# A two-branch kernel on one core: column tiles moved and filled over six rounds, the matrices of the last pass reordered, row endings deferred

## The chip, the core and the metric

The kernel runs on one core of a Trainium2 chip. A core has five engines that run side by side, each through its own stream of instructions in order: PE (TensorE, matrix products; its weight loads are listed as PEld), DVE (VectorE), ACT (ScalarE), POOL (GpSimd) and SP (SyncE, which here only issues transfers). Engines wait for each other through semaphores; 16 DMA engines move data between HBM and the on-chip memory SBUF. PE writes into PSUM, eight banks of 2 KB a partition. The metric is the device time of one execution in microseconds; lower is better.

## The reference

The inputs give two independent results, set side by side in the output (2048 x 2048, bf16).

```python
# A: 64 segments of 32 rows, each with 8 memory rows carried on
for s in range(n_seg):
    h = concat([mem, x[s]]);  q, k, v = h @ Wq, h @ Wk, h @ Wv      # 32 heads of 128
    p = softmax(where(mask, q @ k.T * scale, -1e9));  o = (p @ v) @ Wo
    mem, out[s] = o[:8], o[8:]
# B: a long convolution, its kernel from 128 complex exponentials per channel
K = einsum('dn,dnl,dn->dl', C, exp(dt*A * l), dt*B).real            # 1024 channels, 2048 lags
y = irfft(rfft(u, 4096) * rfft(K, 4096))[:2048] + u * Dskip
```

Both the kernel's spectra and those of the input `u` are made by matrix products with cosine and sine matrices here, not by an FFT.

## The kernel before, in words

Branch B (`part_b`) runs first, then A (`part_a`). Branch B has four stages.

*Parameters.* Tables of exponents and angles are made; the transform's matrix `MF` and the transposes of A's input are made beside them.

*Rounds.* Loop `f` from -1 to 16 (L1270) runs a list of words, `ORDER`, and each word issues one small step; a prime means "of the round before". Rounds 0 to 15 each treat 64 channels: eight exponentials on ACT (words E0 to E7, tile `E`, from PE's `pa`), turns on DVE (n0 to n7, `nr` from `ptt`), sine and cosine on ACT (S, C), products on DVE (gi, gr), the kernel values on PE (K0, K1) and their copy into `KxT` on DVE (x0, x1). Words P, U and M fill the rest with side work: P are projections of branch A, U are transforms of `u`, M transposes matrices. A run word issues PE's part, its small letter the copy out of PSUM: on ACT for p0, p2, p3, p5, on DVE for p1, p4. Every fourth U copy ends in six additions on POOL (`ux` from `us`) and a store to HBM (`Ud`). The PSUM tiles of this side work, of K and of the later builds come from one pool of four banks (`take`). At round 16 only a closing list runs, `LAST` (L1269), which finishes round 15's values and starts what follows.

*Columns.* `columns_of_turns` (L1042) makes two small tiles, `g_l` and `g_r`, by POOL iotas, memsets and selections and by DVE arithmetic; it is called once, at round 3. In round 15 `turned_columns` (L1101) transposes them on PE and copies them out (`lhs`, `wts`, `rhs`); it takes the place of the projections, so the words P and p issue it. From these `build` (L1122) makes the matrices of one of four row groups `kc`: 14 steps, each one or two products and a sine or copy on ACT; three of the steps are amplitudes (`amp`). `weighted` (L1148) multiplies a half of the matrices by them on DVE. In the closing list G0 runs nine steps for `kc` = 0, G1 weighs the first half, G2 runs the other five and the first spectrum on PE, G3 weighs the second half and runs its spectrum, then issues two loads for block 1.

After the list, the 44 stores of kernel values from `KxT` to HBM (`Kd`) that `late` still holds are issued in turn on SP and POOL (L1329), and the pools of the rounds are closed (L1337): from the constants upward `tabs` (tables, columns, staged tiles), `kxp` (two `KxT`) and `tmp` (the rounds' tiles), and from the other end `up` (tiles of the U side). New pools are opened in the memory that they leave: `mnp`, `iv`, `bp`, `pw` (tiles `y` and `z`) and `bp0` on one side, `a_wre1` (tile `k1`, whose upper part holds the amplitudes of the later builds, and the inverse matrices `MI`) on the other. A pool that takes memory of a closed one waits, at its first use, for whatever still reads there.

*Blocks.* Loop `b` from 0 to 15 (L1458). `pointwise` multiplies the spectrum of the values, from two PSUM tiles `hps`, by that of `u` (`uq`, loaded two blocks ahead) on DVE: four instructions into `z` and `y`, at the second `next` four more, which write `Bt`. Between them PE makes the spectrum of the next block, two halves of 20 products, into `hps` tiles from a pool of three. From block 4 on, `inverses(2)` follows: `inverse` (L1426) makes 32 products from `MI` and `Bt` into `yp` on PE, scales them to `yb` on ACT (two buffers), and then DVE ends the row: `uu` times `Dskip`, plus `yb`. The store of `uu` is put on a list, `unsent`, and issued on ACT's queue in a later `inverse`. The row tiles `uu` are loaded six inverses ahead on SP, nine buffers. Eight inverses are left after the loop. Weights of branch A are loaded beside the blocks as memory comes free.

Branch A then loops over 64 segments with part of its weights resident and the rest streamed (tile `wst`).

All engines follow the order in which the program issues their instructions.

Of the kernel before, what the change touches and what calls it, by code (L numbers as in the profile page):

```python
# [10 lines left out]
BF16 = mybir.dt.bfloat16  # L11
# [651 lines left out]
def part_b(ctx, tc, u, A_re, A_im, B_re, B_im, C_re, C_im, log_dt, Dskip, out_b, ahead, copies, residents, first_state):  # L663
# [378 lines left out]
    def columns_of_turns():  # L1042

        at = tabs.tile([128, 6], I32, name="g_at")
        for j, (b0, step) in enumerate(((0, 2), (256, 2), (512, 4), (1024, 8), (2048, 16), (0, 2))):
            gp.iota(at[:, j:j + 1], pattern=[[1, 1]], base=b0, channel_multiplier=step)
        atF = tabs.tile([128, 6], F32, name="g_atF")
        v.tensor_copy(out=atF[:], in_=at[:])

        def select(t_, dims, fill, base, cm):  # L1050
            gp.affine_select(out=t_, in_=t_, compare_op=ALU.is_ge, fill=float(fill), base=base, pattern=[[0, n_] for n_ in dims], channel_multiplier=cm)
# [4 lines left out]
        v.tensor_copy(out=at[:], in_=atF[:])  # L1056
        hl = tabs.tile([128, 2, 6], I32, name="g_hl")
        v.tensor_scalar(out=hl[:, 0, :], in0=at[:], scalar1=6, scalar2=None, op0=ALU.logical_shift_right)
        v.tensor_scalar(out=hl[:, 1, :], in0=at[:], scalar1=63, scalar2=None, op0=ALU.bitwise_and)
        for i, (lo, n_) in enumerate(((0, 2), (2, 3))):  # L1060
            v.tensor_copy(out=g_l[:, 0:10, lo:lo + n_].rearrange("p (s j) c -> p s j c", s=2),
                          in_=hl[:, i, 0:5].unsqueeze(1).unsqueeze(3).to_broadcast([128, 2, 5, n_]))
            v.tensor_copy(out=g_l[:, 10, lo:lo + n_], in_=hl[:, i, 5:6].to_broadcast([128, n_]))
        gp.memset(g_l[:, 0:11, 5:6], 1.0)
        gp.memset(g_l[:, 0:11, 6:7], 0.25)
        gp.memset(g_l[:, 5:10, 6:7], 0.0)
        pn = tabs.tile([128, 4], I32, name="g_pn")
        gp.iota(pn[:, 0:1], pattern=[[1, 1]], base=0, channel_multiplier=1)
        v.tensor_scalar(out=pn[:, 1:2], in0=pn[:, 0:1], scalar1=1, scalar2=None, op0=ALU.bitwise_and)
        v.tensor_scalar(out=pn[:, 2:3], in0=pn[:, 0:1], scalar1=4, scalar2=None, op0=ALU.logical_shift_right)  # L1070
        v.tensor_scalar(out=pn[:, 3:4], in0=pn[:, 0:1], scalar1=15, scalar2=None, op0=ALU.bitwise_and)
        pnF = tabs.tile([128, 5], F32, name="g_pnF")
        v.tensor_copy(out=pnF[:, 0:4], in_=pn[:])
        gp.memset(g_l[:, 11:14, :], 0.0)
        gp.memset(g_l[:, 11:14, 0:1], 1.0)
        gp.memset(g_l[:, 12:14, 1:2], 2.0)
        gp.memset(g_l[:, 13:14, 2:4], 2.0)
        for i, j in ((0, 1), (1, 2), (2, 4)):
            v.tensor_scalar(out=g_l[:, 11 + i, j:j + 1], in0=pnF[:, 1:2], scalar1=-2.0, scalar2=2.0, op0=ALU.mult, op1=ALU.add)
        select(g_l[:, 11:13, 0:5], (2, 5), 0, -1, 1)  # L1080
        select(g_l[:, 13:14, 4:5], (1, 1), 0, -1, 1)
        gp.memset(g_l[:, 11:13, 5:6], 2.0)
        gp.memset(g_l[:, 12:13, 6:7], 2.0)
        select(g_l[:, 11:13, 5:7], (2, 2), 0, 0, -1)
        kq = tabs.tile([128, 2, 16], I32, name="g_kq")
        gp.iota(kq[:, 0, :], pattern=[[1, 4], [0, 4]], base=0, channel_multiplier=0)
        gp.iota(kq[:, 1, :], pattern=[[0, 4], [1, 4]], base=0, channel_multiplier=0)
        kqF = tabs.tile([128, 2, 16], F32, name="g_kqF")
        v.tensor_copy(out=kqF[:], in_=kq[:])
# [5 lines left out]
        v.tensor_scalar(out=rv[:, :, 4], in0=kqF[:, 1, :], scalar1=1.0 / 8, scalar2=0.0, op0=ALU.mult, op1=ALU.add)  # L1095
        gp.memset(g_r[:, :, :, 5:6], 128.0)
        gp.memset(g_r[:, :, :, 6:7], 1.0)

    G = {}

    def turned_columns():  # L1101

        for i in range(4):
            pt = take([128, 8, 128], BF16, "gt")
            for c in range(8 if i != 1 else 6):
                pe.transpose(out=pt[0:7, c, :], in_=g_l[:, 8 * i + c, :] if i < 2 else g_r[:, 2 * (i - 2) + c // 4, c % 4, :], identity=ident[:])

            def evict(copy, i=i, pt=pt):
                flat = pt[0:7].rearrange("p c n -> p (c n)")
                if i == 0:  # L1110
                    copy(out=G["lhs"][:, 0:1024], in_=flat)
                elif i == 1:
                    copy(out=G["lhs"][:, 1024:1408], in_=flat[:, 0:384])
                    copy(out=G["wts"], in_=flat[:, 384:768])
                else:
                    copy(out=G["rhs"][:, 1024 * (i - 2):1024 * (i - 2) + 1024], in_=flat)
            yield evict

# [147 lines left out]
    for eng, names in ((sc.copy, ON_ACT), (v.tensor_copy, ON_DVE)):  # L1266
        for nm, kind, slot in names:
            evict_of[nm] = (kind, slot, eng)
    LAST = ("w0' b0' C0' b1' gi0' C1' G0 gr0' w1' gr1' gi1' K0' K1' G1 x0' x1' G2 M0 G3 m0").split()  # L1269
    for f in range(-1, 17):  # L1270
        if f == 3:
            columns_of_turns()
        if f == 15:
# [13 lines left out]
        for word in ORDER if f < 16 else LAST:  # L1287
            nm, r = word.rstrip("'"), f - word.endswith("'")
            if f == 16 and nm[0] in "GMm" and not word.endswith("'"):
                if nm == "G0":  # L1290
                    for _ in range(9):
                        next(made)
                elif nm == "G1":
                    weighted(0, 0, amp0)
                elif nm == "G2":
                    for _ in made:
                        pass
                    s0 = ps_e.tile([128, 2, 512], F32, name="pa", tag="pa")
# [127 lines left out]
    def inverse(dq, c, uu, neg, mn):  # L1426
# [11 lines left out]
        sc.activation(out=yb[:], in_=yp, func=ACT.Copy, scale=float(2.0 / PLEN))  # L1438
        while len(unsent) > (1 if len(todo) > 6 else 0):
            unsent.pop(0)()  # L1440
        v.tensor_tensor(out=uu[:], in0=uu[:], in1=Dsk[:, d].unsqueeze(1).to_broadcast([128, 2, DQ]), op=ALU.mult)
        v.tensor_tensor(out=uu[:], in0=uu[:], in1=yb[:], op=ALU.add)
        unsent.append(lambda: sc.dma_start(out=out_v[r][:, mc:mc + 2, d], in_=uu[:]))

# [13 lines left out]
    for b in range(16):  # L1458
# [3 lines left out]
        points = pointwise(b, now)  # L1462
        next(points)
        if b == 0:
            ctx_p.close()
# [214 lines left out]
```

## Time and profile before

| what | value |
|---|---|
| runs | 2044.19, 2046.65, 2042.81 us, median 2044.19 |
| profiled execution | time 2047.62 us, span 2045.9 us, mean PE clock 0.975 |
| PE / DVE / ACT / POOL busy | 1834.5 / 1411.2 / 958.1 / 415.3 us |
| HBM read, written | 528.25 MB, 66.05 MB |

Times in the trace count from the start of the span. An instruction's row gives its start, its duration, engine, line, operation, the tile written and the tile read with their shapes, and in brackets how long the engine stood idle ahead of it and for whom. A row of waits gives the waiting engine and line, the releaser, the total, the number and the longest. A row of groups gives count, busy time and mean nanoseconds. A row of stages gives, for a stretch, each engine's busy time, the granted PE clock (1.00 is full), the share of DMA time and GB/s.

### The profile page before, as it was taken

What the parts mean: (1) busy time and instruction counts of PE and PEld (TensorE: products, weight loads), DVE (VectorE), ACT (ScalarE), POOL (GpSimd) and SP (SyncE); (2) the same over time, 40 slices, a digit from 0 to 9 for tenths busy, and PEclk for the clock granted to TensorE, in tenths of its full rate; (3) what the DMA queues carried; (4) which work ended last, traced back from release to release, by engine and by line L of the source; (5) the groups of instructions that cost most, each with busy time, mean ns of one, the idle gap of its engine ahead of it and who ended that gap; (6) DMA issues with size and microseconds to landing.
All of it is one profiled execution on the core that took longest, in us unless ns stands there. A gap on an engine that the chain in (4) does not pass through costs nothing.

```text
span 2045.9 us, 74541 instructions
## 1 busy us (share of the span) xinstructions
PE 1834.5 (90%) x31928; PEld 1130.4 (55%) x31956; DVE 1411.2 (69%) x3442; ACT 958.1 (47%) x1672; POOL 415.3 (20%) x851
## 2 busy tenths in 40 slices
PE   1698999866999879999999999999999999999998
PEld 1365666644877535555555555555555555555554
DVE  8878999958887346666766667666666666666650
ACT  4887988862222324443444444444434444344430
POOL 2135454442200011111111111111111111111121
PEclk9999999977999979999999999999999999999999
DMA  6787997746446999999999999999999999999991
GB/s 169 185 227 227 274 269 202 200 139 212 158 141 203 316 325 339 340 341 340 344 348 332 339 335 358 344 343 344 350 325 350 342 339 341 345 347 344 345 339 50
DMA packets 348469, 588.69 MB, mean 288 GB/s; under 512 B 109865, under 2 KB 225913, under 8 KB 346089
## 3 DMA queue, kind: packets, MB, share of 16 engines
q1 hardware_dynamic: 294748, 526.35, 76.0%
q10 hardware_dynamic: 44812, 28.26, 4.5%
q0 software_dynamic: 8576, 29.32, 4.0%
q8 instruction: 250, 4.10, 0.8%
q14 instruction: 83, 0.67, 0.1%
HBM read 528.25 MB, written 66.05 MB: 290 GB/s over the span
## 4 chain that ended last, share of the span: by engine, by line
PE 35%; DMA 24%; DVE 4%; issue 1%; ACT 1%; POOL 0%; SPq 0%; POOLq 0%; DVEq 0%; ACTq 0%
PE acc L375 18%; DMA wst<-WD_v 11%; PE pp L488 9%; DMA wst<-WD_o 5%; DMA arena<-PKd 3%; PE pe L625 3%; PE tr L386 2%; DMA wst<-WD_q 2%; DMA wst<-WD_k 2%; PE pv L456 1%; PE pv L460 1%; DVE arena L582 1%; ACT arena L582 1%; PE sc L400 1%; PE tro L588 1%
## 5 line engine op out<-in xcount | busy, mean ns | idle before, releaser
L375 PEld LDWEIGHTS <-a_hT 128*32 128x32 bf16 x12352 | 327.2, 96 | 318.3 <-issue 63.0
L381 ACT CAST arena<-acc 128x512 bf16<-128x512 f32 x384 | 224.7, 585 | 397.6 <-PE acc L375 321.9
L375 PE MATMUL acc<-W,a_hT 128*32 128x512 bf16 x4608 | 334.7, 380 | 2.2 <-issue 1.2
L488 PEld LDWEIGHTS <-arena 128*32 128x32 bf16 x8256 | 216.8, 97 | 86.3 <-issue 62.5
L375 PE MATMUL acc<-wst,a_hT 128*32 128x512 bf16 x2304 | 229.7, 381 | 26.6 <-DMA wst<-WD_v 17.8
L389 POOL COPY arena<-arena 128x128 bf16<-128x128 bf16 x128 | 37.4, 292 | 851.4 <-DMA arena<-PKd 300.3
L296 DVE TENSOR_SCALAR arena<-keep 128x256 int32<-128x256 int32 (+1 forms) x512 | 175.5, 394 | 28.1 <-PE acc L375 26.8
L375 PE MATMUL acc<-gF,a_hT 128*32 128x512 bf16 x2048 | 145.6, 382 | 0.0
L488 PE MATMUL pp<-W_o,arena 128*32 128x256 bf16 x4096 | 139.0, 275 | 6.4 <-DMA W_o<-in_A_Wo_dram 5.1
L168 PE MATMUL pro<-xTl,wsl 128*128 128x512 bf16 x490 | 115.9, 389 | 16.2 <-ACT kst L177 7.9
L415 DVE TENSOR_REDUCE a_mx<-sc 128x4 f32<-128x160 f32 (+1 forms) x192 | 71.6, 373 | 77.5 <-PE sc L403 77.5
L419 ACT ACTIVATE sc<-sc 128x160 f32<-128x160 f32 (+1 forms) x192 | 63.9, 333 | 122.9 <-DVE sc L416 122.1
L503 DVE COPY arena<-tr 128x512 bf16<-128x512 bf16 x64 | 27.2, 425 | 128.3 <-PE tr L386 128.3
L423 DVE TENSOR_REDUCE a_mx<-sc 128x4 f32<-128x160 f32 (+1 forms) x192 | 72.8, 379 | 55.5 <-ACT sc L419 55.1
L1208 ACT ACTIVATE E<-pa 128x648 bf16<-128x648 f32 x128 | 90.9, 710 | 32.2 <-PE pa L1200 27.0
L1423 PE MATMUL yp<-Bt,MI 128*128 128x256 bf16 x680 | 104.6, 273 | 0.7 <-ACT yb L1438 0.7
L450 POOL TENSOR_TENSOR arena<-arena,a_BD 128x128 bf16<-128x128 bf16 x128 | 51.0, 399 | 234.9 <-DVE arena L433 218.5
L168 PEld LDWEIGHTS <-wsl 128*128 128x128 bf16 x512 | 51.1, 100 | 77.7 <-issue 23.3
L582 ACT CAST arena<-pp 128x128 bf16<-128x128 f32 x64 | 17.0, 265 | 161.3 <-DVE arena L582 161.3
L375 PE MATMUL acc<-W_v,a_hT 128*32 128x512 bf16 x1280 | 92.3, 381 | 0.0
L1216 DVE TENSOR_SCALAR nr<-ptt 128x456 f32<-128x456 int16 x128 | 77.3, 624 | 17.7 <-PE ptt L1194 16.0
L386 PEld LDWEIGHTS <-arena 128*128 128x128 bf16 x1024 | 57.8, 98 | 54.5 <-issue 44.9
(311 smaller groups left out, 3866.5 us busy)
## 6 DMA issues: line engine op xcount, KB each, us to landing
wst<-WD_v SPq DMA_DIRECT2D x256, 512.0 KB
wst<-WD_k SPq DMA_DIRECT2D x192, 512.0 KB
wst<-WD_o SPq DMA_DIRECT2D x192, 512.0 KB
wst<-WD_q SPq DMA_DIRECT2D x128, 512.0 KB
Ud<-ux POOLq DMA_DIRECT2D x16, 1024.0 KB, 6.1
uq<-Ud SPq DMA_DIRECT2D x32, 512.0 KB
wsl<-in_A_Wk_dram SPq DMA_DIRECT2D x16, 512.0 KB
wsl<-in_A_Wv_dram SPq DMA_DIRECT2D x16, 512.0 KB
```

Of the source, the lines that this page charges most:

```text
L168: nc.tensor.matmul(a[:], lhsT=w[:, kc, 128 * j:128 * j + 128], rhs=xTl[:, kc, :, :].rearrange("p s k -> p (s k)"), start=(kc == 0), stop=( ...
L296: nc.vector.tensor_scalar(out=out.bitcast(I32), in0=in_.bitcast(I32), scalar1=0, scalar2=None, op0=ALU.bitwise_or)
L375: nc.tensor.matmul(a[32 * g:32 * g + 32, o_:o_ + rhs.shape[1]], lhsT=hT[:, kc, :], rhs=rhs, start=(kc == 0), stop=(kc == KC - 1), tile_pos ...
L381: nc.scalar.copy(out=q, in_=a[:])
L386: nc.tensor.transpose(out=p[:, hl, :, :].rearrange("p a b -> p (a b)"), in_=q[:, 128 * hl:128 * hl + 128], identity=ident[:])
L415: nc.vector.tensor_reduce(out=m_, in_=x, axis=AX.X, op=ALU.max)
L419: nc.scalar.activation(out=flat(sc, i), in_=flat(sc, i), func=ACT.Exp, scale=scale)
L423: nc.vector.tensor_reduce(out=m_, in_=x, axis=AX.X, op=ALU.add)
L488: nc.tensor.matmul(po[32 * qt:32 * qt + 32, o_:o_ + rhs.shape[1]], lhsT=oT[:, h % 4, (h % 16) // 4, :], rhs=rhs, start=False, stop=(h == 3 ...
L1208: sc.activation(out=T["E", r, e // 4][:, lo:lo + 8 * NE].rearrange("p (i c) -> p i c", i=2), in_=T.pop(("p", r, e))[:, :, 0:4 * NE], func= ...
L1216: v.tensor_scalar(out=T["n", r, e // 4][:, lo:lo + 8 * NT], in0=T.pop(("t", r, e))[:, 0:8 * NT].bitcast(I16)[:, 0:16 * NT:2], scalar1=floa ...
L1423: pe.matmul(yp[:, b, :], lhsT=m_[:, b, cs, kc, :], rhs=Bt[:, kc, j, half, c_, :], start=(kc == 0 and cs == 0 and half == 0), stop=(kc == 3 ...
```

## The change

Four things, all in `part_b`.

1. `g_l` and `g_r` and the seven small tiles that feed them leave the pool `tabs` for the pool `up`, on the other side of the memory.
2. `columns_of_turns` becomes a generator of six steps: POOL's constants, DVE's first part, POOL's selections, and three DVE parts; one step is issued at the start of each of rounds 1 to 6. `turned_columns` is no longer run by the words P and p: its six steps follow the words E1 to E6 of round 15, each copy is issued at once, the first two transposed tiles are copied by DVE, the others by ACT in two halves each.
3. The closing list: all 14 build steps at G0, G1 ahead of K0', x0' ahead of K1', and the copy of the last U tile, until now at the end of round 15, behind x1'.
4. In `inverse` the two DVE instructions that end a row become a function, kept in the list `endings`; `end()` runs what is kept behind the first part of the next block's `pointwise`, and in the last eight inverses behind each one. All stores on `unsent` are issued at the next `inverse`.

```diff
-    g_l = tabs.tile([128, 14, 7], BF16, name="g_l")
-    g_r = tabs.tile([128, 4, 4, 7], BF16, name="g_r")
...
+    g_l = up.tile([128, 14, 7], BF16, name="g_l")
+    g_r = up.tile([128, 4, 4, 7], BF16, name="g_r")
...
     def columns_of_turns():
-        at = tabs.tile([128, 6], I32, name="g_at")
...
+        at, pn, kq, hl = (up.tile([128, *dims], I32, name="g_%s" % nm) for nm, dims in (("at", (6,)), ("pn", (4,)), ("kq", (2, 16)), ("hl", (2, 6))))
+        atF, pnF, kqF = (up.tile([128, *dims], F32, name="g_%sF" % nm) for nm, dims in (("at", (6,)), ("pn", (5,)), ("kq", (2, 16))))
         for j, (b0, step) in enumerate(((0, 2), (256, 2), (512, 4), (1024, 8), (2048, 16), (0, 2))):
             gp.iota(at[:, j:j + 1], pattern=[[1, 1]], base=b0, channel_multiplier=step)
...
+        gp.memset(g_r[:, :, :, 6:7], 1.0)
+        yield
         v.tensor_copy(out=atF[:], in_=at[:])
...
+            v.tensor_scalar(out=g_l[:, 11 + i, j:j + 1], in0=pnF[:, 1:2], scalar1=-2.0, scalar2=2.0, op0=ALU.mult, op1=ALU.add)
+        yield
...
         select(g_l[:, 13:14, 4:5], (1, 1), 0, -1, 1)
+        yield
...
     def turned_columns():
...
-            def evict(copy, i=i, pt=pt):
...
-            yield evict
+            if i == 0:
+                v.tensor_copy(out=G["lhs"][:, 0:1024], in_=flat)
+            elif i == 1:
+                v.tensor_copy(out=G["lhs"][:, 1024:1408], in_=flat[:, 0:384])
+                v.tensor_copy(out=G["wts"], in_=flat[:, 384:768])
+            else:
+                for h in range(2):
+                    sc.copy(out=G["rhs"][:, 1024 * (i - 2) + 512 * h:1024 * (i - 2) + 512 * h + 512], in_=flat[:, 512 * h:512 * h + 512])
+                    yield
+                continue
+            yield
...
-    LAST = ("w0' b0' C0' b1' gi0' C1' G0 gr0' w1' gr1' gi1' K0' K1' G1 x0' x1' G2 M0 G3 m0").split()
+    LAST = ("w0' b0' C0' b1' gi0' C1' G0 gr0' w1' gr1' gi1' G1 K0' x0' K1' x1' U3 G2 M0 G3 m0").split()
+    steps = columns_of_turns()
     for f in range(-1, 17):
-        if f == 3:
-            columns_of_turns()
+        if 1 <= f <= 6:
+            next(steps)
...
-            side_ops["P"] = (turned_columns(),)
+            turning = turned_columns()
...
+            if f == 16 and nm == "U3":
+                run_evict("U", 3, v.tensor_copy)
...
                 if nm == "G0":
-                    for _ in range(9):
-                        next(made)
+                    for _ in made:
+                        pass
...
-                if f == 15 and nm == "m":
-                    run_evict("U", 3, v.tensor_copy)
...
+                elif f == 15 and nm in ("E1", "E2", "E3", "E4", "E5", "E6"):
+                    next(turning)
...
-        while len(unsent) > (1 if len(todo) > 6 else 0):
+        while unsent:
             unsent.pop(0)()
...
+        def ending():
+            v.tensor_tensor(out=uu[:], in0=uu[:], in1=Dsk[:, d].unsqueeze(1).to_broadcast([128, 2, DQ]), op=ALU.mult)
+            v.tensor_tensor(out=uu[:], in0=uu[:], in1=yb[:], op=ALU.add)
+            unsent.append(lambda: sc.dma_start(out=out_v[r][:, mc:mc + 2, d], in_=uu[:]))
+        endings.append(ending)
...
+    def end():
+        while endings:
+            endings.pop(0)()
...
         next(points)
+        end()
...
     ctx2.close()
+    end()
     for n_ in range(8):
         inverses(1)
+        end()
```

More of the change, by code (lines that the diff above doesn't have):

```diff
@@ L1045, in columns_of_turns @@
         for j, (b0, step) in enumerate(((0, 2), (256, 2), (512, 4), (1024, 8), (2048, 16), (0, 2))):
             gp.iota(at[:, j:j + 1], pattern=[[1, 1]], base=b0, channel_multiplier=step)
[L1047 to L1051, printed above, removed]
+        gp.iota(pn[:, 0:1], pattern=[[1, 1]], base=0, channel_multiplier=1)
@@ new lines, in columns_of_turns @@
+        gp.memset(g_l[:, 12:13, 6:7], 2.0)
+        select(g_l[:, 11:13, 5:7], (2, 2), 0, 0, -1)
+        gp.memset(g_r[:, :, :, 5:6], 128.0)
+        gp.memset(g_r[:, :, :, 6:7], 1.0)
+        yield
+        v.tensor_copy(out=atF[:], in_=at[:])
+        v.tensor_scalar(out=pn[:, 1:2], in0=pn[:, 0:1], scalar1=1, scalar2=None, op0=ALU.bitwise_and)
+        v.tensor_scalar(out=pn[:, 2:3], in0=pn[:, 0:1], scalar1=4, scalar2=None, op0=ALU.logical_shift_right)
+        v.tensor_scalar(out=pn[:, 3:4], in0=pn[:, 0:1], scalar1=15, scalar2=None, op0=ALU.bitwise_and)
@@ L1052, in columns_of_turns @@
+        v.tensor_copy(out=pnF[:, 0:4], in_=pn[:])
+        v.tensor_copy(out=kqF[:], in_=kq[:])
+        for i, j in ((0, 1), (1, 2), (2, 4)):
+            v.tensor_scalar(out=g_l[:, 11 + i, j:j + 1], in0=pnF[:, 1:2], scalar1=-2.0, scalar2=2.0, op0=ALU.mult, op1=ALU.add)
+        yield
         for j, fill in ((2, 513), (3, 1025), (4, 2050)):
@@ L1095, in columns_of_turns @@
         v.tensor_scalar(out=rv[:, :, 4], in0=kqF[:, 1, :], scalar1=1.0 / 8, scalar2=0.0, op0=ALU.mult, op1=ALU.add)
-        gp.memset(g_r[:, :, :, 5:6], 128.0)
-        gp.memset(g_r[:, :, :, 6:7], 1.0)
+        yield
+        v.tensor_copy(out=at[:], in_=atF[:])
+        v.tensor_scalar(out=hl[:, 0, :], in0=at[:], scalar1=6, scalar2=None, op0=ALU.logical_shift_right)
+        v.tensor_scalar(out=hl[:, 1, :], in0=at[:], scalar1=63, scalar2=None, op0=ALU.bitwise_and)
+        yield
+        for i, (lo, n_) in enumerate(((0, 2), (2, 3))):
+            v.tensor_copy(out=g_l[:, 0:10, lo:lo + n_].rearrange("p (s j) c -> p s j c", s=2),
+                          in_=hl[:, i, 0:5].unsqueeze(1).unsqueeze(3).to_broadcast([128, 2, 5, n_]))
+            v.tensor_copy(out=g_l[:, 10, lo:lo + n_], in_=hl[:, i, 5:6].to_broadcast([128, n_]))
+        yield
     G = {}
@@ L1295, in part_b @@
                 elif nm == "G2":
-                    for _ in made:
-                        pass
                     s0 = ps_e.tile([128, 2, 512], F32, name="pa", tag="pa")
```

61 lines of the change are left out of this document (17 added, 44 removed).

## The prediction

> **What bounds the kernel now.** I read the page's busy shares first, then a table of stages, then the waits and the timeline of each stage that the diff touches.
>
> ```profile
> span 2045.9 us, 74541 instructions
> PE 1834.5 (90%) x31928; PEld 1130.4 (55%) x31956; DVE 1411.2 (69%) x3442; ACT 958.1 (47%) x1672; POOL 415.3 (20%) x851
> ```
> ```profile
> core 0: us, PE busy (x) PEld busy (x) DVE busy (x) ACT busy (x) POOL busy (x), PEclk, DMA share, GB/s
> 200.00:399.90 199.90, 199.13 (x2584) 134.78 (x2595) 186.61 (x291) 178.85 (x201) 101.05 (x122) 1.00 0.85 236
> 404.20:427.00 22.80, 13.61 (x216) 9.28 (x213) 19.27 (x32) 18.97 (x21) 6.35 (x8) 0.85 0.79 255
> 427.00:447.00 20.00, 10.17 (x163) 6.23 (x162) 15.57 (x16) 11.93 (x17) 9.80 (x7) 0.55 0.19 73
> 447.00:467.00 20.00, 12.14 (x67) 6.83 (x66) 0.06 (x1) 10.65 (x21) 11.60 (x21) 0.67 0.30 79
> 526.90:645.90 119.00, 107.24 (x954) 91.18 (x954) 97.10 (x111) 28.98 (x32) 0.00 (x0) 1.00 0.54 167
> 666.00:742.00 76.00, 55.69 (x642) 36.13 (x640) 23.92 (x64) 20.15 (x31) 2.80 (x8) 0.85 0.94 336
> 760.00:2030.00 1270.00, 1211.81 (x25167) 700.18 (x25169) 820.00 (x2561) 510.55 (x1124) 202.15 (x507) 1.00 0.94 334
> ```
>
> In the steady rounds PE has no slack (199.1 of 199.9 us) and DVE 7%, so a delay on DVE reaches PE. In the last round (404 to 427), in the closing pass and the hand-over to the blocks (427 to 467) no engine is full: these are waits. In the blocks with inverses PE has 107 of 119 us. The attention, from 760 on, is untouched and starts when the blocks end. So each stall taken away before 700 us should move the end by its own length, unless the loading at 666 to 742, with the DMA engines 94% busy, eats it.
>
> **The columns over six rounds.** Now all of it stands at the start of round 3:
>
> ```profile
> 157.17 0.68 DVE L946 COPY ms<-mt 128x1024 bf16<-128x1024 bf16 x1
> 159.46 0.17 DVE L1048 CAST g_atF<-g_at 128x6 f32<-128x6 int32 x1 [1.61 <-POOL g_at L1046]
> 160.58 0.17 DVE L1056 CAST g_at<-g_atF 128x6 int32<-128x6 f32 x1 [0.95 <-POOL g_atF L1051]
> 163.21 0.18 DVE L1089 CAST g_kqF<-g_kq 128x32 f32<-128x32 int32 x1 [1.05 <-POOL g_kq L1087]
> 163.73 0.19 DVE L1095 TENSOR_SCALAR g_r<-g_kqF 128x16 bf16<-128x16 f32 x1
> 169.26 3.44 PE L168 MATMUL pro<-xTl,wsl 128*128 128x512 bf16 x8 [4.93 <-ACT kst L177]
> ```
> ```profile
> DVE wn L1234 <- ACT sn L1221: 2.3, 10, 0.2
> ```
>
> DVE waits three times for POOL (3.6 us) and computes 22 small instructions; it is held from 157.85, the end of the copy ahead, to 163.92. PE pays 4.93 us at 169.26. Afterwards POOL's part stands a round ahead, so the three waits go; its 21 instructions in round 1 and 7 selections in round 3 (0.1 to 0.2 us each; POOL is half idle in the rounds) delay only loads of parameters that are used a round later. The DVE instructions stay: about 1.2 us in round 2, 0.6 in round 4, 0.5 in 5, 0.4 in 6, from their starts in the timeline. Each round has 0.2 us free there (the wait for the sine). Since nearly all of the held time reached PE, I charge the rest: 1.0+0.4+0.3+0.2 = 1.9 us. Net **-3.0 us** (ends -4.9, if small pieces vanish in gaps, and -2.0, if they pull further waits along).
>
> **The turned columns in round 15.** 30 transposes and their copies move from the place of the projections to behind the exponentials E1 to E6.
>
> ```profile
> 412.12 0.70 PE L1200 MATMUL pa<-RE,pt 128*128 128x324 bf16 x2 [7.70 <-ACT E L1208]
> L1116 ACT COPY g<-gt 7x1024 bf16<-7x1024 bf16 x2 | 2.0, 984 | 0.0
> L1111 ACT COPY k<-gt 7x1024 bf16<-7x1024 bf16 x1 | 1.0, 984 | 0.0
> L1106 PE MATMUL gt<-b_ident,g_l 128*7 128x128 bf16 x14 | 0.9, 219 | 0.0
> ```
>
> Three copies of 0.98 us stand on ACT ahead of E0, E1 and E2 while PE waits 7.70 us for E0. Moving them starts E0 0.98 us earlier, and ACT is relieved of one copy (DVE takes it; a 1024-column copy takes DVE about 0.7 us). Against it: the 0.9 us of 14 transposes makes some 2.1 us for 30, now between the exponentials, where PE is on the path; DVE and ACT wait in line for each of them, and behind them stand the turns and products of the same round. The last U copy (two DVE instructions of 0.68 us) leaves the round. I take **-1 us** (ends -3 and +2: copies hidden entirely, or transposes all on the path with DVE's waits).
>
> **The closing pass and the hand-over.** These rows carry it:
>
> ```profile
> 430.39 2.18 DVE L1182 TENSOR_TENSOR gi<-E,sn 128x1824 bf16<-128x1824 bf16 x1
> 440.80 1.04 DVE L1015 CAST KxT<-kp 128x392 bf16<-128x392 f32 x2
> 444.38 0.96 DVE L1151 TENSOR_TENSOR g<-g,amp 128x1536 bf16<-128x1536 bf16 x1 [2.55 <-ACT g L1120]
> 466.94 1.22 DVE L1366 TENSOR_TENSOR z<-uq,pa 128x1024 f32<-128x1024 f32 x1 [21.60 <-DMA Kd<-KxT]
> ```
> ```profile
> L1182 DVE TENSOR_TENSOR gi<-E,sn 128x1824 bf16<-128x1824 bf16 x20 | 22.3, 1116 | 0.0
> PE hps L1171 <- DVE y L1366: 18.8, 2, 11.8
> ```
> ```profile
> 418.71 1.26 POOL L980 TENSOR_TENSOR ux<-us 128x512 f32<-128x512 f32 x1
> 419.93 2.78 POOL L982 TENSOR_TENSOR ux<-us 128x256 f32<-128x256 f32 x4
> 423.16 0.55 POOL L983 DMA_DIRECT2D Ud<-ux  x1 [0.45 <-POOL ux L982]
> 427.51 1.99 POOL L979 TENSOR_TENSOR ux<-us 128x512 f32<-128x512 f32 x1 [2.00 <-DMA Ud<-ux]
> 431.55 5.20 POOL L982 TENSOR_TENSOR ux<-us 128x256 f32<-128x256 f32 x4
> 461.02 4.36 POOL L1022 DMA_DIRECT2D Kd<-KxT  x8 [1.28 <-issue]
> 454.47 1.51 ACT L1142 CAST k<-gf 128x512 bf16<-128x512 f32 x3
> 458.76 2.48 ACT L1120 ACTIVATE gF<-gf 128x512 bf16<-128x512 int16 x5
> ```
>
> The large wait is z: block 0 does not begin until POOL's last store of kernel values, issued up to 465.38, has read KxT. z does not use these values. It writes a new pool whose memory must be free. From the shapes: behind the constants lie tabs (13,376 bytes a partition) and two KxT of 12,544, together 38,464; the later mn, iv and B pools take 8,192+13,696+16,384 = 38,272. So the pool of y and z begins 192 bytes inside the second KxT. That the wait goes by address shows in the same rows: ACT writes k1, of a pool opened after the same close but elsewhere, at 454.47 without it. Moving the columns takes 896 bytes (padded) out of tabs; KxT then ends 704 bytes below y. **The wait goes**, though no line of the diff says so.
>
> What is late next: z needs the first spectrum, and the spectrum of block 1 needs the matrices of block 1. PE had issued these when ACT took the last of them (458.76 on), then sat 11.8 us until z and y freed its banks. So PE gains those 11.8 us if the matrices come as before. They begin earlier, but the amplitudes go into k1, over the memory of the U tiles, and the last U copy now stands behind the last kernel values: two DVE instructions, then POOL's six additions (two of 1.26 and four in 2.78 undisturbed, 5.3 us), the store and its landing (423.16 to 427.51, 4.4 us): with the last KxT copy near 441, about as now (the products gain 4 us, but K0' waits for the sines ahead of it), that is 452 to 454, against 454.47 now. So what the earlier spectrum gives, this takes. The gain is **-12 us** (ends -8 and -17: the store lands late, or early and all of the earlier start counts). Moving G1 and the sines of the second half ahead of K0' costs nothing: ACT has them done by about 440 (11 sines and 3 copies of half a microsecond, by the rows at 454.47 and 458.76) while DVE makes gr and gi, which now run without POOL beside them (2.18 against 1.12 us); without that cover K0' would wait some 2 us. SP's 24 stores still follow G3's load; POOL's 20 now stand behind the U additions as they stood behind ms before, so they end at about 465 again, and load_k(1) needs them only in block 2.
>
> Here a rule weighs: the Trainium skill, GPSIMD Engine Reference, Key points, says that GpSimd shares its SBUF interfaces with VectorE and is slowed by instructions with two SBUF inputs. The gi row agrees. By it the additions, now beside z and y (one input in PSUM), run undisturbed; were they disturbed as at 427.51 and 431.55 (3.9 us more for the six), the term would be -8.
>
> **The endings behind the next products.**
>
> ```profile
> PE hps L1171 <- DVE y L1366: 12.3, 10, 1.2
> 525.81 1.22 DVE L1366 TENSOR_TENSOR z<-uq,hps 128x1024 f32<-128x1024 f32 x1
> 532.85 2.36 DVE L1372 TENSOR_TENSOR Bt<-y 128x1024 bf16<-128x1024 f32 x2
> 538.54 0.43 DVE L1442 TENSOR_TENSOR uu<-uu,yb 128x512 bf16<-128x512 bf16 x1 [2.14 <-ACT yb L1438]
> 538.88 1.21 DVE L1366 TENSOR_TENSOR z<-uq,hps 128x1024 f32<-128x1024 f32 x1
> ```
>
> A block takes 13.07 us (525.81 to 538.88). DVE ends with the addition that waits for the second inverse; only then come z and y, which free PE's bank: 1.23 us lost in each of ten blocks. Afterwards z and y go ahead of the endings; their spectrum was ready long before. DVE's work per block, 9.4 us plus four endings of 0.42 less overlap, is 10.9 against PE's 13.07-1.23 = 11.84. Endings wait until 0.65 us after the second inverse T, end at T+2.2, the products at T+6.9; z and y for the next block run from there and end 0.3 us before the next T, while PE asks for the bank 2.35 us after it. yb's two buffers are free at T+1.3, first needed at T+8.3. Stores go out in pairs, one inverse behind their endings; the load that reuses a row tile waits for the same store as before. **-12.3 us** (ends -10 and -13).
>
> Sum: -3.0-1.0-12.0-12.3 = -28.3. On the profiled execution (span 2045.9, time 2047.6) that is 2019.3; the median shown, 2044.19, lies 3.4 below it: **2015.9 us**.
>
> **Rivals.** (a) The loading absorbs the inverses' gain: DMA is 94% busy from 666 to 742. But these loads start when buffers come free at the last spectra, and the share is 0.54 before; so they shift along. If not: 2028. (b) The wait of z stays, or another of its length takes its place (banks, uq): 2028. (c) The last U store holds the amplitudes 4 to 8 us: 2020 to 2024. (d) The PE clock, 0.55 from 427 to 447 and 0.67 to 467, stays full as the gaps shrink: the first spectrum takes 2 us less, and with an early store all goes sooner: 2008 to 2011. The Trainium skill, TensorE: Matmul & The Clock Gate, Part 1, has the clock halve after about 3.4 us of idleness; the 1.23 us gaps at clock 1.00 agree. (e) Slower: the deferred endings put DVE's in-order wait for yb ahead of the second products. If DVE lost its lead, so that points of a block ran wholly after it, PE would stall 6.9 us a block (0.65+1.5+4.8+2.3 less 2.35) instead of 1.23: +57 us, 2085 with the rest. It decides from 2.8 us a block on. Against it: z needs nothing of the inverses.
>
> **How the numbers follow.** Forecast 0.60 (2010 to 2020), (a) 0.08, (b) 0.09, (c) 0.10, (d) 0.06, (e) 0.05, nothing measurable 0.02. The range 2009 to 2028 takes in all but (e), nothing, and part of (a), (b), (d). Under 0.2% (4 us) this kernel's measurement tells no change: faster 0.93, same 0.02, slower 0.05.
>
> **What would show it.** Right: no DVE wait for Kd<-KxT at z, and z some 20 us sooner against the end of the products; no wait of PE for y in blocks 5 to 14, which are 11.8 us apart; rounds 2 to 6 of nearly equal length; the first k1 copy on ACT waiting for Ud<-ux. Wrong: z waiting still, PE waiting for y again, or a longer load stage after the last spectra.

## The result and the profile after

The changed kernel takes 2013.36 us, the median of four runs (2008.12 to 2014.35), against 2045.42 (2042.81 to 2051.64): a ratio of 0.983, with a 95% interval of 0.981 to 0.986. The forecast was 2015.9. The profiled execution took 2013.72 us with a span of 2012.0, which is 33.9 us below the span of before. The forecast's sum was 28.3.

The page's span and busy times, and the table of stages (columns as in the table of before: the stretch, its length, busy times of the five engines, clock, DMA share, GB/s). The stretches are placed by the same work as before, not at the same times.

```profile
span 2012.0 us, 74581 instructions
PE 1830.2 (91%) x31956; PEld 1129.2 (56%) x31956; DVE 1408.8 (70%) x3443; ACT 958.4 (48%) x1673; POOL 417.7 (21%) x851
```
```profile
405.20:424.80 19.60, 15.67 (x239) 10.57 (x239) 12.53 (x22) 11.98 (x19) 6.46 (x8) 0.90 0.52 183
424.80:447.00 22.20, 16.10 (x210) 9.85 (x210) 18.47 (x24) 15.70 (x25) 7.18 (x8) 0.69 0.17 53
447.00:467.00 20.00, 14.36 (x77) 8.29 (x76) 11.94 (x11) 10.07 (x21) 10.19 (x19) 0.66 0.63 183
500.90:619.90 119.00, 119.00 (x1078) 103.71 (x1077) 110.70 (x125) 32.96 (x36) 7.02 (x20) 1.00 0.58 182
633.20:709.20 76.00, 58.68 (x678) 38.67 (x679) 23.31 (x66) 22.22 (x34) 2.80 (x8) 0.85 0.96 342
```

PE's work is the same as before; only idle time has gone. In the blocks with inverses PE now has 119.0 of 119.0 us (before 107.2), and from 447 to 467, where DVE had done 0.06 us of work, it does 11.9. The load stage still takes 76 us with the DMA engines at 0.96.

To see which part of the change earned what, cut the span at instructions that every version has: E0 (the first exponential) of rounds 1, 14 and 15, the copy to -w behind round 15's first sine (the first DVE instruction of the closing pass), the first product z of block 4, and the first matmul of part A (the accumulation at L375). Each length below is the difference of two start times in the trace.

| us | before | after | difference | forecast |
|---|---|---|---|---|
| E0 of round 1 to E0 of round 14 | 266.0 | 259.8 | -6.2 | -3.0 (columns) |
| E0 of round 14 to E0 of round 15 | 20.0 | 20.0 | 0.0 | -1.0 for this |
| E0 of round 15 to the -w behind it | 15.6 | 19.6 | +4.0 | and this line (turned columns) |
| -w to z of block 4 | 84.2 | 70.7 | -13.6 | -12.0 (closing pass, hand-over) |
| z of block 4 to part A | 185.4 | 168.4 | -17.0 | -12.3 (endings) |
| part A to the end | 1349.2 | 1348.1 | -1.1 | 0 |

Three terms gained more than forecast and one had the wrong sign. The errors (-3.2, +5.0, -1.6, -4.7 and -1.1) add to -5.6 and partly hide each other. That the total came so near is partly luck, and it proves none of the terms. The experiments take them one by one.

The rows of after that answer to those of the prediction come from the timeline and from the waits. First the hand-over: z at 440.90 instead of 466.94 and without the wait for Kd<-KxT, then the waits from 424 to 500 (the waiting instruction, what it waited for, us in total, times, longest).

```profile
438.91 1.68 DVE L1152 TENSOR_TENSOR g<-g,amp 128x1536 bf16<-128x1536 bf16 x1
440.90 1.22 DVE L1368 TENSOR_TENSOR z<-uq,pa 128x1024 f32<-128x1024 f32 x1 [0.31 <-PE pa L1172]
```
```profile
DVE gF L1152 <- ACT k L1143: 7.8, 1, 7.8
...
PE gf L1130 <- ACT k L1143: 5.0, 1, 5.0
ACT k L1143 <- DMA MId<-ms: 5.0, 1, 5.0
```

The wait that took its place is the last row: ACT may not write the amplitudes into k1 until POOL's last two stores are through; PE waits 5.0 us for ACT, and DVE 7.8.

And the blocks: one steady block, then all waits of PE between z of block 4 and part A. The ten waits of 1.2 us for y are gone.

```profile
559.12:570.79 11.67, 11.67 (x107) 10.19 (x106) 10.68 (x13) 4.90 (x4) 0.00 (x0) 1.00 0.47 143
```
```profile
PE hps L1425 <- ACT yb L1440: 0.7, 1, 0.7
PE yp L1425 <- ACT mn L1391: 0.5, 1, 0.5
```

### The profile page after: what moved, and what is told of

The parts are those of the page before. It is cut to its first block, busy times and chain, and to the rows that moved or that the text cites. A ratio compares the mean times of both kernels' runs of the same rounds, so it can differ in the third digit from the quotient of the medians.

```text
span 2012.0 us, 74581 instructions
## 1 busy us (share of the span) xinstructions
PE 1830.2 (91%) x31956; PEld 1129.2 (56%) x31956; DVE 1408.8 (70%) x3443; ACT 958.4 (48%) x1673; POOL 417.7 (21%) x851
## 4 chain that ended last, share of the span: by engine, by line
PE 36%; DMA 24%; DVE 3%; issue 1%; ACT 1%; POOL 0%; SPq 0%; POOLq 0%; DVEq 0%
PE acc L375 21%; DMA wst<-WD_v 8%; PE pp L488 7%; DMA wst<-WD_o 7%; DMA wst<-WD_k 4%; DMA arena<-PKd 3%; PE pe L625 3%; PE tr L386 2%; DMA wst<-WD_q 2%; PE sc L400 1%; PE pv L456 1%; DVE arena L582 1%; PE pv L460 1%; ACT arena L582 1%; DVE arena L441 1%
## 5 line engine op out<-in xcount | busy, mean ns | idle before, releaser
L375 PEld LDWEIGHTS <-a_hT 128*32 128x32 bf16 x12352 | 327.5, 96 | 311.6 <-issue 56.5
L375 PE MATMUL acc<-W,a_hT 128*32 128x512 bf16 x4608 | 334.7, 380 | 0.2 <-issue 0.2
L375 PE MATMUL acc<-wst,a_hT 128*32 128x512 bf16 x2304 | 229.7, 382 | 24.1 <-DMA wst<-WD_v 15.2
L375 PE MATMUL acc<-gF,a_hT 128*32 128x512 bf16 x2048 | 145.7, 382 | 0.0
L375 PE MATMUL acc<-W_v,a_hT 128*32 128x512 bf16 x1280 | 92.3, 381 | 0.0
L488 PE MATMUL pp<-wst,arena 128*32 128x256 bf16 x1536 | 76.7, 275 | 13.2 <-DMA wst<-WD_o 12.2
```

What stands on the lines that cost most here:

```text
L375: nc.tensor.matmul(a[32 * g:32 * g + 32, o_:o_ + rhs.shape[1]], lhsT=hT[:, kc, :], rhs=rhs, start=(kc == 0), stop=(kc == KC - 1), tile_pos ...
L488: nc.tensor.matmul(po[32 * qt:32 * qt + 32, o_:o_ + rhs.shape[1]], lhsT=oT[:, h % 4, (h % 16) // 4, :], rhs=rhs, start=False, stop=(h == 3 ...
```

## The experiments

The time of part A alone, whose instructions are the same in all versions, ranges from 1345.8 to 1353.4 us over the fourteen profiled executions here. A term of a few microseconds therefore can't be read from one span, and hardly from a median. It is read from its stage, and the ratio stands beside it.

**Does the address free z?** An unused tile of 736 bytes a partition moves the second KxT back into the pool of y and z. By the addresses of the compiled kernels, 704 bytes would make it end exactly where that pool begins.

```
     par_t = [tabs.tile([128, 8, 128], BF16, name="pt%d" % n_) for n_ in range(2)]
+    tabs.tile([128, 368], BF16, name="pad")
```

> The changed kernel with one unused tile of 736 bytes a partition behind the parameter tiles, so that the second KxT ends 32 bytes inside the pool of y and z (704 bytes would end exactly at it). Theory (the hand-over was freed by the layout): z waits again for POOL's last store of kernel values, issued at about 468, so z's first product goes from 440.9 to about 469.5 and block 1 follows about 19 us later than in the changed kernel: about 2032 us (2028 to 2036). Rival (the order of the closing pass or the earlier matrices took the wait away): the tile changes nothing, 2013 us.

The second kernel also shifts y by 64 bytes within its pool.

```
     pw = ctx2.enter_context(tc.tile_pool(name="b_pw", bufs=1))
+    pw.tile([128, 32], BF16, name="fill")
```

> The same 736 bytes, and 64 unused bytes at the head of the pool of y and z, so that the pool begins 32 bytes inside KxT but y itself 32 bytes behind it. If a wait for memory goes by the tile: no wait, 2013 us. If it goes by the whole pool: as with 736 bytes alone, about 2032 us.

Timeline rows of z, of the first kernel and then of the second:

```profile
464.21 1.22 DVE L1369 TENSOR_TENSOR z<-uq,pa 128x1024 f32<-128x1024 f32 x1 [25.77 <-DMA Kd<-KxT]
```
```profile
466.60 1.22 DVE L1370 TENSOR_TENSOR z<-uq,pa 128x1024 f32<-128x1024 f32 x1 [27.30 <-DMA Kd<-KxT]
```

Thirty-two bytes bring the whole wait back, with the order of the closing pass unchanged, so the order did not remove it. The second kernel waits as well although y itself lies clear of KxT: the wait goes by the pool, not by the tile. The instruction that waits says the same in the kernel before and in the first of these two: it writes z, which lies behind all of y in its pool and so clear of KxT. From -w to z of block 4 they take 85.7 and 87.3 us (changed kernel 70.7). I had expected 19 us and it is 15 and 16.6, because during the wait PE finishes matrices of block 1 that it otherwise makes behind z. The ratios are 0.988 (0.985 to 0.991) and 0.989 (0.986 to 0.993).

**Is the layout enough?** The kernel before, with only the pool of the columns' tiles changed (at, atF, hl, pn, pnF, kq and kqF like the two shown):

```
-    g_l = tabs.tile([128, 14, 7], BF16, name="g_l")
-    g_r = tabs.tile([128, 4, 4, 7], BF16, name="g_r")
...
+    g_l = up.tile([128, 14, 7], BF16, name="g_l")
+    g_r = up.tile([128, 4, 4, 7], BF16, name="g_r")
```

> The kernel before with its columns' tiles allocated in the other pool, and nothing else: same instructions in the same order. Theory (layout alone frees z): z goes right behind the last kernel values, at about 444 instead of 466.94, the 11.8 us of PE in front of the spectrum of block 1 go, and the next limit is the amplitudes at 454.5: about 2033.6 us, that is 11.8 below before (2031 to 2036). Rival (the new order of the closing pass or the late last U copy is needed too): less than half of that, 2040 or more.

```profile
438.28 0.57 POOL L983 DMA_DIRECT2D Ud<-ux  x1 [0.41 <-POOL ux L982]
...
448.45 1.22 DVE L1366 TENSOR_TENSOR z<-uq,pa 128x1024 f32<-128x1024 f32 x1 [1.99 <-PE pa L1171]
...
450.32 0.56 POOL L947 DMA_DIRECT2D MId<-ms  x1 [11.47 <-ACT ms L946]
...
454.26 1.55 ACT L1142 CAST k<-gf 128x512 bf16<-128x512 f32 x3
```

z waits 1.99 us for PE and no longer for a store (the other rows are used further down). The stage falls from 84.2 to 71.2, that is by 13.0 of the change's 13.6 us, without a moved instruction. The time is 0.992 of before (0.989 to 0.995), the median 2036.3 against 2033.6 expected. So the new order of the closing pass, though x1' ends 1.9 us sooner behind -w (12.9 instead of 14.8), adds only 0.6.

**Where did the order's own gain go?** Into the wait for the last stores. The amplitudes go elsewhere:

```
-    amp = k1[:, 2560:4096]
+    amp = mnp.tile([128, 2, 2, 4, 128], BF16, name="mn", tag="mn")[:].rearrange("p a b c d -> p (a b c d)")[:, 0:1536]
```

> The changed kernel with the amplitudes of blocks 1 to 3 in a tile of the pool of negated inverse matrices (free there until block 4, and beginning where the tables lay) instead of in k1. Theory (the first amplitude copy waits 5.0 us for the last store of U): the wait goes, the copy starts at about 446.8 instead of 451.8, PE's idle of 5.0 us before 452.5 goes, and the end moves by 4 to 5 us: about 2009 us. Rival (another wait stands right behind: the sines, the loads or the weighting): within 1.5 us of the changed kernel, 2012 to 2013.

From the timelines: POOL's last two stores and the first amplitude copy in the changed kernel, and below it z of block 0, the copies and z of block 1 in this one:

```profile
444.94 0.56 POOL L983 DMA_DIRECT2D Ud<-ux  x1 [0.41 <-POOL ux L982]
445.54 0.56 POOL L947 DMA_DIRECT2D MId<-ms  x1
...
451.82 0.59 ACT L1143 CAST k<-gf 128x512 bf16<-128x512 f32 x1 [5.01 <-DMA MId<-ms]
```
```profile
440.88 1.22 DVE L1368 TENSOR_TENSOR z<-uq,pa 128x1024 f32<-128x1024 f32 x1 [0.27 <-PE pa L1172]
...
446.69 1.51 ACT L1143 CAST mn<-gf 128x512 bf16<-128x512 f32 x3
...
456.60 1.22 DVE L1368 TENSOR_TENSOR z<-uq,hps 128x1024 f32<-128x1024 f32 x1 [0.33 <-PE hps L1172]
```

In the changed kernel the copy starts behind the two stores; here 5.1 us sooner and without a wait. z of block 1 comes 4.8 us sooner (461.42 before this edit), and 3.6 of it reach block 4 (67.1 instead of 70.7). The forecast's sentence, that what the earlier spectrum gives the store takes, is shown by this. The ratio is 0.978 (0.974 to 0.981). That is further below the changed kernel's than 3.6 us explain; in the profiled run the stage's gain is met by a part A of 1350.8 us, and the span is 2011.0.

**The endings alone**, on the kernel before, as the change has them (the two operations on uu and the store's entry in unsent go into the new function):

```
+        def ending():
...
+        endings.append(ending)
...
         next(points)
+        end()
```

> The kernel before with the inverses' endings behind the next products, and nothing else. From block 4 to the first matmul of part A the trace of the changed kernel is 17.0 us shorter than before, where ten idles of 1.23 us explain 12.3. Theory (all of it comes from the endings: the idles, the shorter wait at their side, and the inverses after block 15): that stretch is 16 to 17 us shorter than before, about 2029 us. Rival (4 to 5 us of it come from the earlier start, loads having landed by then): 12 to 13 us shorter, about 2033 us.

Two rows of its table of stages (z of block 4 to z of block 15, and on to part A), and below them the same two stretches of before:

```profile
510.94:635.64 124.70, 124.70 (x1130) 108.84 (x1128) 116.13 (x130) 32.96 (x36) 11.37 (x41) 1.00 0.61 196
635.64:679.56 43.92, 42.72 (x378) 36.06 (x375) 17.95 (x32) 16.05 (x19) 0.00 (x0) 1.00 0.82 285
```
```profile
511.22:657.74 146.52, 133.57 (x1192) 114.05 (x1190) 118.49 (x135) 34.79 (x40) 11.59 (x41) 1.00 0.54 172
657.74:696.65 38.91, 35.94 (x316) 30.02 (x315) 16.50 (x28) 13.34 (x16) 0.00 (x0) 1.00 0.82 277
```

The two stretches together take 168.6 us instead of 185.4, that is 16.8 less, so all but 0.2 us of the 17.0 is the endings' own, and nothing that can be seen comes from an earlier start. The ratio is 0.991 (0.988 to 0.994).

**The columns alone**, on the kernel before, tiles where they were:

```
+    steps = columns_of_turns()
     for f in range(-1, 17):
-        if f == 3:
-            columns_of_turns()
+        if 1 <= f <= 6:
+            next(steps)
```

> The kernel before with the filling of the columns' tiles over rounds 1 to 6, their tiles where they were. Theory (small pieces vanish in gaps, and the transposes' and projections' place behind the long stop goes with it): the exponential E0 of round 14 comes 6 us earlier, about 2039.5 us. Rival (the prediction's charge of 1.9 us for the pieces that stay): 3 us. In both the wait of z for the kernel values' stores stays.

E0 of round 1 to E0 of round 14 takes 259.9 us, 6.1 less than before (the changed kernel 6.2 less); the ratio is 0.997 (0.994 to 1.000). From E0 to E0, rounds 1 to 4 take 19.95, 25.36, 21.21 and 19.94 us before, and here 20.46, 19.95, 19.95 and 19.95. So the stop was worth 5.4, the round behind it 1.3, and the pieces cost 0.5, in one round only. Why the round behind it was long stands in two rows of the kernel before, the stop and what follows it:

```profile
169.40:172.80 3.40, 3.40 (x10) 1.25 (x9) 3.40 (x6) 2.42 (x3) 0.00 (x0) 0.51 0.96 206
165.00:169.40 4.40, 0.14 (x1) 0.10 (x1) 4.29 (x7) 4.04 (x4) 2.38 (x3) 1.00 0.94 214
```

PE stands nearly still from 165.0 to 169.4 and then runs at a granted clock of 0.51 for 3.4 us. Half of 3.4 us is 1.7, of which 1.3 arrive. The layout kernel, which has the same stop, shows that this price follows the clock: behind an idle of 4.96 us of PE its granted clock is 0.50 from 168.79 to 172.19 and still 0.64 on to 175.60, and the round behind the stop takes 22.39 us there, 2.4 more than a steady one instead of 1.3.

**The turned columns back at the projections' places**, in the changed kernel:

```
-            turning = turned_columns()
+            side_ops["P"] = (turned_columns(),)
...
-                elif f == 15 and nm in ("E1", "E2", "E3", "E4", "E5", "E6"):
-                    next(turning)
```

> The changed kernel with the turned columns' transposes and copies of round 15 where they were, at the projections' places and on their engines. Theory (behind the exponentials the copy of the first transposed tile makes VectorE wait 3.5 us for PE behind E0, and the round loses 4.0 us): from E0 of round 15 to the next -w the time goes from 19.7 back to about 15.6 us, with E0 a microsecond later, so 3 us in all. Rival (the round's loss is the half clock of 399 to 409, which stays as PE's idle stays): less than 1 us.

and with two of the four copies moved once more:

```
-            side_ops["P"] = (turned_columns(),)
+            turning = turned_columns()
+            side_ops["P"] = (itertools.islice(turning, 3),)
...
+            if f == 16 and nm == "T3":
+                next(turning)(sc.copy)
...
-                run_evict(*evict_of[nm])
+                kind, slot, eng = evict_of[nm]
+                run_evict(kind, slot, v.tensor_copy if f == 15 and nm == "p3" else eng)
```

(T3 stands behind G1 in the closing pass.)

> As the one before, but the first copy of transposed columns on VectorE instead of ScalarE, and the last tile (for blocks 2 and 3) transposed and copied in the closing pass while ScalarE is idle. Theory (E0 waits for a row of copies of 0.98 us on ScalarE ahead of it): E0 comes 1 us earlier than there, the round is 1 to 2 us shorter again, 4 to 5 us below the changed kernel. Rival (VectorE's own line is as full, or the late copy delays the matrices): no better than the one before.

Waits from 396 to 424 in the changed kernel, and in the first of these two:

```profile
ACT E L1209 <- PE pa L1201: 3.8, 3, 2.5
DVE k L1109 <- PE gt L1106: 3.5, 1, 3.5
ACT E L1209 <- DVE gi L1184: 2.2, 1, 2.2
```
```profile
ACT E L1208 <- PE pa L1200: 2.2, 3, 1.0
```

In the first fence DVE waits for the transposes and ACT's exponentials for PE and DVE. In the second, of these only ACT's wait for PE is left, and shorter: E0 of round 15 to -w is 15.6 us, 4.0 less. That is the theory's figure for this stretch, and the rival fell: behind E0 the granted clock is 0.50 for about the same time in both (405.24 to 409.3 in the changed kernel, 404.04 to 407.8 here), so it is not what makes the 4.0 us. The theory's other half fell too: E0 does not come a microsecond later (20.0 us from E0 to E0 in both). The second kernel took a copy of 0.98 us from ACT ahead of E0 and gained nothing either: 20.0 and 15.6, and its late copy made x1' end 0.8 us later behind -w. The ratios, 0.982 (0.978 to 0.987) and 0.982 (0.979 to 0.986), can't tell 4 us from none. What E0 does wait for is in the timeline of before:

```profile
409.07 0.98 ACT L1111 COPY k<-gt 7x1024 bf16<-7x1024 bf16 x1
409.35 0.58 DVE L1183 TENSOR_TENSOR gr<-E,nr 128x768 bf16<-128x768 bf16 x1
...
410.07 1.28 ACT L1208 ACT_TABLE_LOAD   x1
```
```profile
403.26 0.58 DVE L1184 TENSOR_TENSOR gr<-E,nr 128x768 bf16<-128x768 bf16 x1
403.94 1.28 ACT L1209 ACT_TABLE_LOAD   x1 [0.87 <-DVE gr L1184]
```

Before, the copy on ACT ends at 410.05, but the product gr, which reads the tile that E0 overwrites, ends at 409.93. After (second fence) the copy is gone, ACT idles 0.87 us, and the table load stands behind the end of gr just the same. The copy was hidden by DVE.

**Both repairs together**, that is the edit of the amplitudes and the first of the two just shown, against the changed kernel on the same chip, twice:

> The changed kernel once more, as the partner of the next one on the same chip: 0.983 of before, its stages as in the first profile (19.6 us from E0 of round 15 to the next -w, 70.7 from there to block 4's z, 168.4 to part A).

> The changed kernel with both repairs: the amplitudes of blocks 1 to 3 in the pool of negated matrices, and the turned columns of round 15 at the projections' places. Theory (two waits in a row on one chain: 4.0 us of round 15 and 3.6 us between there and block 4): their savings add, 7.6 us below the changed kernel in the stages up to part A, about 2005.5 us, 0.979 to 0.980 of before. Rival (the second takes up the first, since the earlier round only lengthens the next wait): 3.5 to 5 us, 2009 us.

> The changed kernel a third time, partner of the next one: part A begins at about 663.7 us and lasts 1347 to 1350 us.

> The kernel with both repairs a second time. Its part A began 8.4 us earlier than the changed kernel's and lasted 5.0 us longer in the first profile. Theory (scatter: in the profiles so far that stretch lasts 1345.8 to 1353.4 us without any trend in where it begins): its length falls within 2 us of the partner's, and the time is 6 to 9 us below it. Rival (the attention's loads give back what comes earlier than 660): again some 5 us longer, and 3 to 4 us below the partner.

Rows of the first pair, changed kernel and then both repairs: E0 of round 15 to -w, on to z of block 4, on to part A.

```profile
405.28:424.73 19.45, 15.50 (x239) 10.47 (x239) 12.53 (x22) 12.01 (x18) 6.45 (x8) 0.90 0.53 183
424.73:495.15 70.42, 50.99 (x413) 32.11 (x413) 56.33 (x59) 33.28 (x60) 24.79 (x39) 0.71 0.60 194
495.15:663.62 168.47, 167.27 (x1505) 144.81 (x1504) 134.16 (x161) 49.10 (x55) 11.38 (x41) 1.00 0.66 216
```
```profile
404.06:419.58 15.52, 12.89 (x209) 8.98 (x209) 11.22 (x19) 11.83 (x16) 6.43 (x8) 0.88 0.72 245
419.58:486.47 66.89, 52.47 (x411) 32.56 (x411) 56.50 (x58) 33.17 (x60) 24.94 (x39) 0.72 0.61 198
486.47:655.20 168.73, 167.53 (x1507) 145.02 (x1505) 134.16 (x161) 49.01 (x55) 11.38 (x41) 1.00 0.67 218
```

The savings add: 3.9 and 3.5 us in the first pair (third stage +0.3), 3.5 and 4.6 in the second (20.4 to 16.9 and 71.4 to 66.8; third stage -1.4). That the first of these stages is about a microsecond longer in both kernels of the second pair goes with the clock: behind E0 it is 0.50 for 6.1 us (changed kernel) and 6.7 us (both repairs) there, and for 3.7 and 3.6 us in the first pair. The times are 2012.82 and 2009.24 us in the first pair (ratios to before 0.982, 0.980 to 0.985, and 0.981, 0.978 to 0.983) and 2017.48 and 2006.04 in the second (0.987, 0.984 to 0.989, and 0.981, 0.979 to 0.984). By the stages from E0 of round 1 to part A the gain is 7.1 and 9.7 us, and the mean of the two differences in time is 7.5, against 7.6 expected; the single differences of 3.6 and 11.4 show how little one pair settles. Part A was 5.0 us longer in the first pair and 0.2 in the second, so it was scatter that took part of the first pair's gain, and not loads of the attention that give back what comes early. The version with both repairs has the lower median in both pairs, though within a pair the intervals overlap or just meet; and the edit of the amplitudes alone, on another chip, had a ratio to before of 0.978, so the times don't rank these kernels.

## Why the prediction was right, and where it was wrong

**The columns.** The mechanism was right and the size too small: -6.2 for -3.0, outside the ends (-4.9 to -2.0). Three terms were mis-sized. The pieces were charged 1.9 us over four rounds and cost 0.5 in one. The half clock behind the stop, 1.3 us of the next round, was not in the sum at all. And the stop was taken at 4.9 us, the idle of PE alone, where its round lost 5.4. The Trainium skill, TensorE: Matmul & The Clock Gate, Part 1, gives the rule (the clock halves after about 3.4 us of idleness); the rows agree: a stop of 4.93 us, then 3.4 us at 0.51. I had used the rule for the hand-over and not here.

**The turned columns in round 15.** This step was wrong: +4.0 for -1, outside the ends (-3 to +2). "Moving them starts E0 0.98 us earlier" failed, because I read ACT's order of instructions as the cause of its time. E0 was bound by gr on DVE, which ended 0.12 us before the copy did. And the upper end of +2 named DVE's waits, but it is no larger than the 2.1 us of the transposes themselves. The line behind them got no price: DVE's in-order wait of 3.5 us for the first transposed tile, with its turns and products queued behind, which held ACT's exponentials in turn.

**The closing pass and the hand-over.** Right, with its inner argument: the wait of z went by the layout (pad and layout kernels), and a store took the place (-13.6 for -12, within -8 to -17). Three details differ. The wait goes by pools: by the addresses of the compiled kernels k1's amplitudes lie over the tables' products, not over the tiles of U, and it is k1's pool that reaches over those. And the trace names the store of matrices (`MId` from `ms`, in the same pool as the tiles of U), issued 0.6 us behind that of U, as the last to land. Whether U's additions and store are at the bottom of it is only an estimate: `ms` was ready at 442.36 but POOL was still at the additions, and in the kernel before and the layout kernel, where U's store had gone 12 to 13 us ahead, the matrices' store landed in 2.6 and 3.8 us. By that it would have landed by about 446.2 here, ahead of 446.8, when ACT was free for the copy. The layout kernel's copy doesn't settle it: it shows no wait, but its store, issued at 450.32, had landed 0.1 us before the copy began at 454.26. No run moves U's store alone. And "moving G1 and the sines of the second half ahead of K0' costs nothing" failed:

```profile
433.23 2.50 PE L1130 MATMUL gf<-g,k 7*128 7x256 bf16 x10
433.36 0.56 DVE L1184 TENSOR_TENSOR gi<-E,wn 128x768 bf16<-128x768 bf16 x1
...
435.65 0.23 PE L1007 MATMUL kp<-gr 128*32 128x49 bf16 x4
```

DVE has the last product at 433.92, but PE first works off the ten angle products moved ahead of K0' and begins K0' at 435.65, 1.7 us later. The cover, gr and gi on DVE, was gone sooner than I had it, since they run without POOL beside them (gi in 1.12 us). The prediction had priced that case at 2 us and then excluded it; no run here moves G1 back alone.

**The endings.** Right in mechanism, -17.0 for -12.3, beyond the end of -13. The sum counted only the row of ten waits for y. These three rows of before, in the waits of PE between block 4 and part A, were not counted, though the same reordering takes most of them:

```profile
PE yp L1423 <- ACT mn L1389: 2.3, 2, 1.3
PE hps L1423 <- ACT yb L1438: 0.7, 1, 0.7
PE yp L1423 <- ACT yb L1438: 0.7, 1, 0.7
```

Before, PE's waits there were 12.3 + 3.7 = 16.0 us; afterwards 1.2 are left, so 14.8 went. The other 2.3 us are PE's own busy time in the trace (169.5 us before, 167.2 after): a steady block's 107 matmuls take 11.84 us with an idle in them and 11.67 without.

**The rivals.** (a) fell: part A begins 32.8 us sooner and lasts 1.1 us less. (b) is what the kernel with the pad shows. (c) is what happened, but at the forecast's own price. (d) came without its gain: the clock is 0.69 from 424.8 to 447 (0.55 from 427 to 447 before), but behind that the amplitudes wait for the stores, and from 447 to 467 it is 0.66 against 0.67. (e) did not occur: no row has PE waiting for y in these blocks.

## What to carry to other kernels

An allocation moved out of a pool shifts everything behind it, and a wait for memory goes by the pool's range: in the padded kernel 32 bytes brought 15 us back, and in the change itself 896 bytes moved elsewhere took such a wait away, with no line of the diff about it. Add up the addresses before believing that a reordering removed a wait. A small copy put behind an engine's wait costs what is queued behind it on an in-order engine; to price it, follow the queue, not the copy. And cut the span at instructions that all versions share: a total that came out nearly right had one term of the wrong sign.

## What the runs showed of the hardware that was not expected

A store of 256 KB issued 0.6 us behind one of 1024 KB on the same queue took as long to land as the large one, though it took 2.6 us in the kernel before (issued at 450.16) and 3.8 in the layout kernel, 12 to 13 us behind the store of U (DMA view of the changed kernel, 440 to 455; KB each, median us from issue to landing):

```profile
Ud<-ux POOLq DMA_DIRECT2D x1, 1024.0 KB, 5.9
...
MId<-ms POOLq DMA_DIRECT2D x1, 256.0 KB, 6.2
```

A block became 1.40 us shorter (13.07 to 11.67) though the idle that went was 1.23 us: the other 0.17 us were in PE's busy time, with the clock at 1.00 in both. Ends of matmuls are modelled in the trace, so the block's length is the safer figure.

GpSimd's additions of U and DVE's weighting slow each other when they overlap, as if they took turns. The first addition, already under way when the weighting began (row at 438.91 above), took 1.29 us against 1.26 in the kernel before (418.71). The weighting took 1.68 us instead of 0.96, 0.72 more, and 0.86 of the first addition were left when it began. The second addition took 2.00 us, 0.74 more, and 0.85 of the weighting were left when it began. In the kernel with the pad, where z comes 25 us later, it took 2.03, so z is not the cause. The four additions beside z and y took 2.83 against 2.78.

```profile
438.48 1.29 POOL L979 TENSOR_TENSOR ux<-us 128x512 f32<-128x512 f32 x1 [15.10 <-DVE us L974]
439.74 2.00 POOL L980 TENSOR_TENSOR ux<-us 128x512 f32<-128x512 f32 x1
441.70 2.83 POOL L982 TENSOR_TENSOR ux<-us 128x256 f32<-128x256 f32 x4
```

The Trainium skill, GPSIMD Engine Reference, Key points, names this contention for VectorE instructions with two SBUF inputs, and the weighting is one. That z and y, with one input in PSUM, left the additions undisturbed is what the prediction took from it, and the trace agrees.
